# A long convolution by matrix transforms: from 64 by 64 points on the whole array to 128 by 32 points on its four quarters

## The chip, the cores and the metric

The kernel runs on one core of one Trainium2 chip. The metric is device time in microseconds, the median of several runs. The names in the traces are PE for TensorE, PEld for TensorE's weight loads, DVE for VectorE, ACT for ScalarE, POOL for GpSimd and SP for SyncE, which issues nearly all DMAs here.

## The reference

Sequence length 2048, 512 channels, all in fp32. Two kinds of layer alternate, A B A B, each after a layer norm over the channels, each with a long causal convolution per channel:

```python
def _A_ref(q, k, v, shift_k, ssm_k, ssm_D):
    ...                                   # k_shift: short causal convolution of k, 4 taps
    kv = k_shift * v
    y = irfft(rfft(kv padded to 2S) * rfft(ssm_k padded to 2S))[:S]
    y = y + kv * ssm_D
    return q * y
def _B_ref(u, log_A_real, A_imag, C_real, C_imag, log_dt, D_skip):
    ...
    P = jnp.exp((A * dt[:, None])[:, :, None] * pos[None, None, :])
    K = 2.0 * jnp.einsum("dn,dnl->dl", C, P).real      # 128 modes a channel, 2048 taps
    y = irfft(rfft(u padded) * rfft(K padded))[:L]
    return y + u * D_skip
x = x + _A_ref(_layernorm(x), A_k, A_v, A_shift_k, A_ssm_k, A_ssm_D)
x = x + _B_ref(_layernorm(x), B_...)
x = x + _A_ref(_layernorm(x), ...)                    # the same weights, k and v again
x = x + _B_ref(_layernorm(x), ...)
return x
```

The convolution inside layer A does not depend on x, so it is done once and its result is used twice. There are three long convolutions in all (A's, and B's twice), and two spectra of kernels (A's given taps, B's generated taps).

## The kernel before, in words

**Transform.** A 4096-point real transform is done in two matrix steps. The first step (`fwd_rows`, `fwd_group`, L171; tile `pf`) multiplies 128-partition data by a constant 128 by 128 matrix. In layer A, in both spectra, and in the first groups of layer B that matrix is `wz`, half of whose rows are zeros, so that each of the two halves of the partitions is picked out in turn; elsewhere in layer B 64-row halves of `w1` are used. VectorE transposes the result in blocks (L193, L195) into `z`. The second step (`f2_chunk`, L200; tile `pu`) multiplies by one 128 by 128 matrix of `w2` for each of 32 frequencies, four frequencies a chunk, 8 chunks a quarter of 128 channels. `spectrum_quarter` does both steps for a kernel's taps, adds `D` as a bias to tap 0 by a one-row matmul (L187), copies the chunks out of PSUM (L245, tile `pc`) and stores them in DRAM (`spec`, L246).

**Product and inverse.** `convolution` walks over 32 chunks (4 quarters of channels by 8). For each it loads the chunk of the spectrum twice, real part and imaginary part on all partitions (`kab`, L260), runs `f2_chunk`, has ScalarE make a swapped and negated copy of `pu` in two halves (`sw`, L277 and L278), VectorE multiply `pu` by `kab` (`vv`, L279), GpSimd multiply `sw` by `kab` (L281), and GpSimd or, every third time in layer B, VectorE add the two (L282). `lag` chunks later the inverse's first step (L291; tile `pi`) multiplies `vv` by `mm`, ScalarE copies it to `ie` (L292), VectorE transposes (L306, tile `w`), and the last step (L312; tile `po`, two 64-column tiles of the array) is followed by `finish`.

**Order.** Two generators of program steps are interleaved by `run_steps`. `stream` makes layer B's taps (64 steps of `mags`, `angles`, `waves`, `products`, `contract`; L467 to L520) and, as each quarter is complete, its spectrum. `diagonal` makes layer A's spectrum, the gated input (`gated`), and runs layer A's convolution. Then `gated_update` applies A to x (L715 to L724), layer B's convolution runs, `gated_update` again, and layer B's convolution for the second time, ending with the stores of `out` (L816). Within an engine a scheduler places the instructions by its own timeline, so `pu`, `pf` and the generator's matmuls mix.

**Buffers.** While A's convolution and the generator run, PSUM has three banks for `pf`, `pu`, `pi` and `po` (tag `c1`), two for `pm` and the second spectrum, two for `pa` and one for `pk`. In layer B there are four banks for `pu`, `pi`, `po` and two double banks for `pf`.

Of the kernel before, what the change touches and what calls it, by code (L numbers as in the profile page):

```python
# [20 lines left out]
NQ = 4  # L21
CK = 4
NCH = 32 // CK
# [8 lines left out]

def dft_constants():
    c = lambda t: np.cos(2 * np.pi * t)
    s = lambda t: np.sin(2 * np.pi * t)
    n1 = np.arange(32)
    k2 = np.arange(64)
    j = np.arange(32)
    n2 = [32 * (j // 16) + 16 * b + j % 16 for b in range(2)]
    w1 = np.zeros((2, 32, 2, 2, 32))  # L40
    w4 = np.zeros((2, 2, 32, 2, 32))
    w2 = np.zeros((32, 2, 2, 32, 2, 64))
    for b in range(2):
        w1[b, :, b, 0, 0] = 1
        w1[b, :, b, 1, 0] = (-1.0) ** n1
        w4[b, 0, 0, b] = 1 / NFFT
        w4[b, 1, 0, b] = (-1.0) ** n1 / NFFT
        m = n2[b][:, None]
        for k in range(1, 32):
            w1[b, :, b, 0, k] = c(n1 * k % 64 / 64)  # L50
            w1[b, :, b, 1, k] = -s(n1 * k % 64 / 64)
            w4[b, 0, k, b] = 2 * c(n1 * k % 64 / 64) / NFFT
            w4[b, 1, k, b] = -2 * s(n1 * k % 64 / 64) / NFFT
            ph = m * (k + 64 * k2)[None, :] % NFFT / NFFT
            w2[k, b, 0, :, 0], w2[k, b, 0, :, 1] = c(ph), -s(ph)
            w2[k, b, 1, :, 0], w2[k, b, 1, :, 1] = s(ph), c(ph)
        for q in range(32):
            ph = m[:, 0] * (64 * q) % NFFT / NFFT
            w2[0, b, 0, :, 0, q] = c(ph)
            if q > 0:  # L60
                w2[0, b, 0, :, 1, q] = -s(ph)
            ph = m[:, 0] * (32 + 64 * q) % NFFT / NFFT
            w2[0, b, 1, :, 0, 32 + q], w2[0, b, 1, :, 1, 32 + q] = c(ph), -s(ph)
        w2[0, b, 0, :, 1, 0] = (-1.0) ** m[:, 0]
    w2 = w2.reshape(32, 128, 128)
    mm = w2.transpose(0, 2, 1).copy()
    mm[0].reshape(2, 64, 128)[:, 1:] *= 2.0
    w1 = w1.reshape(64, 128)
    f = lambda a: np.ascontiguousarray(a, dtype=np.float32)
    return {  # L70
        "w1": f(np.concatenate([w1, w1])),
        "w2": f(w2.transpose(1, 0, 2)),
        "mm": f(mm.transpose(1, 0, 2)),
        "w4": f(w4.reshape(128, 64)),
    }
# [24 lines left out]
def kernel(ctx: ExitStack, tc: tile.TileContext, out, x_in, kv_in, ssmk_in, ssmd_in,  # L100
                           la_in, ai_in, cr_in, ci_in, ldt_in, ldtb_in, dsk_in,
                           w1_in, w2_in, mm_in, w4_in, minus_in, tt_in, tg1_in, tg2_in, dbg=None):
# [12 lines left out]
    spec = [[dram.tile([NCH, 128, CK * 128], F32, name=f"spec{i}_{q}") for q in range(NQ)] for i in range(2)]  # L115
# [7 lines left out]
    LV = 0  # L123
# [11 lines left out]
    wz = cpool.tile([128, 2, 128], F32, name="wz")  # L135
    w2 = cpool.tile([128, 32, 128], F32, name="w2")
    mm = cpool.tile([128, 32, 128], F32, name="mm")
# [5 lines left out]
    psum, w1, swapped = {}, [], [None]  # L143

    def bank(name, tag="c1"):
        pool, bufs = psum[tag]
        return pool.tile([128, 512], F32, name=name, tag=tag, bufs=bufs)


# [4 lines left out]
    def wide_bank():  # L154
        pool, bufs = psum["f1"]
        return pool.tile([128, 2, 512], F32, name="pf", tag="f1", bufs=bufs).rearrange(
            "p a (x t r) -> p a x t r", t=16, r=2)


    def fwd_rows(src, pf, j, step, rows, full):  # L160
        for a in (1, 0):
            half = slice(0, 128) if full else slice(64 * a, 64 * a + 64)
            w = wz[:, a, :] if full else w1[0][half, :]
            rhs = src(half, j, step)[:, rows, :]
            o = pf[:, a].rearrange("p x t r -> p t x r")[:, rows]
# [5 lines left out]
            yield T.matmul(o, w, rhs, start=True, stop=True)  # L171

    def fwd_group(src, z, c0, n, step, tap0=None, first=None, tag="c1", full=True, early=None):
        for j in range(0, n, step):
            rest = slice(0, 16)
            if early is not None:
                pf, rest = early, slice(8, 16)
            elif step == 32:
                pf = wide_bank()
            else:  # L180
                both = bank("pf", tag).rearrange("p (x n r) -> p x r n", n=32, r=2)
                pf = both.rearrange("p x r (a t) -> p a x t r", a=2)
            for i in fwd_rows(src, pf, j, step, rest, full):
                if first is not None:
                    after(i, first)
            if tap0 is not None:
                T.matmul(pf[:, 0, :, 0, :], wz[0:1, 0, :],  # L187
                         tap0[:, j:j + step].rearrange("p (x r) -> p x r", r=2), start=False, stop=True,
                         skip_group_check=True)
            zr = z[:, (c0 + j) // 2:(c0 + j + step) // 2].rearrange("p x k r -> p x r k")  # L190
            if step == 32:
                for r in range(2):
                    V.transpose(zr[:, :, r], pf[..., r].rearrange("p a x t -> p x a t"))  # L193
# [722 lines left out]
```

## Time and profile before

| | |
|---|---|
| median of 3 runs | 797.05 us (791.2 to 798.05) |
| the profiled execution | 802.01 us, its span 800.2 us |
| mean granted TensorE clock | 0.862 of full |
| DMA | 135.49 MB, mean 169 GB/s |

The profile lists each engine's busy time, groups of instructions by line with their mean duration, and a chain of work that ended last. One matmul of fp32 data appears as two PE instructions and two weight loads, so a chunk of four matmuls is "x8". A group's mean duration includes the time an instruction waits in the array's pipeline behind its predecessor; the spacing of starts is shorter, and is read from pieces of the chain.

### The profile page before, as it was taken

The page shows a single profiled execution, that of the slowest core. Times are in us where ns is not written, and L with a number is a line of the kernel's source. Part 1 is how long each engine was busy: PE and PEld are TensorE (multiplying, and loading weights), DVE is VectorE, ACT ScalarE, POOL GpSimd, SP SyncE. Part 2 cuts the span into 40 slices and gives each one's busy share as a digit, 9 for nine tenths or more (in the row PEclk, how much of TensorE's full clock was granted, in tenths as well). Part 3 has the DMA queues.
Part 4 walks back from the last instruction along what each step waited for, and adds up shares of the span by engine and source line. Part 5 has one row for each costly group of instructions (what it writes and reads, how often), then busy time and mean ns, then how long its engine had stood idle before and what let it go on. Part 6 is the DMA issues. An engine that isn't in the chain of part 4 may idle for free.

```text
span 800.2 us, 14659 instructions
## 1 busy us (share of the span) xinstructions
PE 676.5 (85%) x5192; PEld 475.6 (59%) x5192; DVE 604.8 (76%) x939; ACT 479.2 (60%) x881; POOL 531.9 (66%) x464
## 2 busy tenths in 40 slices
PE   3779988999989999999899867889789840898996
PEld 2555755667667766757666444666557720476673
DVE  7767856989996958756849699625568989878775
ACT  4144443535478884785884687628746625878572
POOL 4966744967868975777964678206666836288783
PEclk9686765869999999999999755699989975999998
DMA  9586254557378463664541891238968541078792
GB/s 329 195 263 249 94 174 151 187 171 253 130 222 231 131 184 97 192 187 153 125 119 54 268 313 42 76 115 206 238 169 197 147 106 53 1 182 220 200 247 99
DMA packets 89614, 135.49 MB, mean 169 GB/s; under 512 B 8509, under 2 KB 37701, under 8 KB 89029
## 3 DMA queue, kind: packets, MB, share of 16 engines
q1 hardware_dynamic: 88644, 132.13, 56.8%
q0 software_dynamic: 896, 2.43, 1.0%
q8 instruction: 41, 0.67, 0.4%
q14 instruction: 33, 0.26, 0.1%
HBM read 98.87 MB, written 35.65 MB: 168 GB/s over the span
## 4 chain that ended last, share of the span: by engine, by line
PE 27%; DVE 14%; ACT 4%; DMA 4%; issue 3%; POOL 2%; SPq 1%; DVEq 0%; POOLq 0%; ACTq 0%
PE pu L200 8%; PE pf L171 6%; PE pi L291 5%; PE po L312 5%; DVE x L722 3%; DVE ut L715 2%; DMA kab<-spec 2%; POOL sw L281 1%; DMA yaq<-ya_d 1%; DVE w L306 1%; PE pk L520 1%; DVE vv L279 1%; POOL vv L282 1%; DVE tt L506 1%; DVE st L822 1%
## 5 line engine op out<-in xcount | busy, mean ns | idle before, releaser
L281 POOL TENSOR_TENSOR sw<-sw,kab 128x512 f32<-128x512 f32 x96 | 125.4, 1313 | 76.5 <-ACT sw L278 65.5
L505 POOL TENSOR_TENSOR xy<-tt,m 128x512 f32<-128x512 f32 x64 | 89.7, 1402 | 62.7 <-ACT tt L494 54.6
L200 PEld LDWEIGHTS pu<-zu,w 128*128 128x128 f32 x768 | 94.6, 191 | 51.1 <-DVE vv L279 18.4
L200 PE MATMUL pu<-zu,w 128*128 128x128 f32 x768 | 108.4, 283 | 12.2 <-DVE vv L279 11.8
L171 PE MATMUL pf<-kk,wz 128*128 128x256 f32 x256 | 96.2, 512 | 24.7 <-DMA kk<-ssmk_in 15.9
L279 DVE TENSOR_TENSOR vv<-pu,kab 128x512 f32<-128x512 f32 x96 | 64.7, 679 | 64.6 <-ACT sw L278 32.0
L282 POOL TENSOR_TENSOR vv<-vv,sw 128x512 f32<-128x512 f32 x76 | 100.1, 1320 | 14.8 <-DVE vv L279 12.0
L291 PE MATMUL pi<-vv,mm 128*128 128x128 f32 x768 | 106.9, 284 | 3.4 <-DVE vv L279 2.8
L291 PEld LDWEIGHTS pi<-vv,mm 128*128 128x128 f32 x768 | 95.3, 195 | 15.9 <-issue 9.4
L277 ACT ACTIVATE sw<-pu 64x512 f32<-64x512 f32 x96 | 57.1, 595 | 63.0 <-PE pu L200 52.1
L200 PE MATMUL pu<-zk,w 128*128 128x128 f32 x512 | 80.4, 313 | 5.5 <-DVE zk L195 3.6
L492 ACT ACTIVATE tt<-pa 128x512 f32<-128x512 f32 x64 | 38.5, 601 | 75.4 <-PE pa L484 64.1
L200 PEld LDWEIGHTS pu<-zk,w 128*128 128x128 f32 x512 | 74.8, 223 | 14.4 <-DVE zk L195 4.1
L171 PEld LDWEIGHTS pf<-kk,wz 128*128 128x128 f32 x256 | 57.8, 247 | 42.8 <-issue 16.0
L245 ACT COPY pc<-pu 128x512 f32<-128x512 f32 x64 | 37.5, 592 | 63.1 <-PE pu L200 45.7
L469 ACT ACTIVATE m<-pm 128x512 f32<-128x512 f32 x96 | 54.2, 598 | 31.5 <-PE pm L467 30.6
L506 DVE TENSOR_TENSOR tt<-tt,m 128x512 f32<-128x512 f32 x64 | 71.6, 1118 | 0.4
L507 DVE SCALAR_TENSOR_TENSOR xy<-tt,m 128x256 f32<-128x256 f32 x64 | 51.1, 798 | 24.0 <-ACT tt L493 20.2
L195 DVE STREAM_TRANSPOSE zk<-pf 128x512 f32<-128x512 f32 x64 | 44.5, 703 | 28.0 <-PE pf L187 27.8
L312 PE MATMUL po<-w,w 128*64 128x512 f32 x192 | 56.1, 671 | 7.8 <-DVE w L306 6.7
L509 POOL TENSOR_TENSOR xy<-tt,m 128x256 f32<-128x256 f32 x64 | 60.9, 951 | 0.0
L520 PE MATMUL pk<-xy,tt 128*32 128x64 f32 x2048 | 53.7, 244 | 5.8 <-POOL xy L509 3.1
(141 smaller groups left out, 1310.3 us busy)
## 6 DMA issues: line engine op xcount, KB each, us to landing
kab<-spec SPq DMA_DIRECT2D x188, 256.0 KB, 4.0
spec<-pc SPq DMA_DIRECT2D x64, 256.0 KB, 2.4
kvt<-kv_in SPq DMA_DIRECT2D x16, 624.0 KB, 6.5
yaq<-ya_d SPq DMA_DIRECT2D x8, 1024.0 KB, 5.5
kk<-ssmk_in SPq DMA_DIRECT2D x16, 256.0 KB, 5.1
kv_d<-u SPq DMA_DIRECT2D x16, 256.0 KB
kdram<-ks SPq DMA_DIRECT2D x64, 64.0 KB, 2.4
kk<-kdram SPq DMA_DIRECT2D x16, 256.0 KB, 2.6
```

The source lines that it names most:

```text
L171: yield T.matmul(o, w, rhs, start=True, stop=True)
L200: ins = T.matmul(pu[:, i, :], w2[:, c * CK + i, :], z[:, :, c * CK + i, :], start=True, stop=True)
L277: S.mul(sw[0:64], pu[64:128], -1.0)
L279: V.tensor_mul(vv, pu, kabs[s][:, 0])
L281: (V if last else G).tensor_mul(sw, sw, kabs[s][:, 1])
L282: (V if last or s % add_dve == add_dve - 1 else G).tensor_add(vv, vv, sw)
L291: i1s[t] = T.matmul(pi[:, i, :], mm[:, c * CK + i, :], vvs[t][:, i, :], start=True, stop=True)
L312: ins = T.matmul(po[64 * a:64 * a + 64], w4, ws[g][:, :, 16 * a:16 * a + 16, :].rearrange("p x t r -> p t x r"), start=True, stop=True, ti ...
L505: G.tensor_mul(xy[:, :, :, 32:64], tt[:, :, :, 1:33], m1[:, :, 32:64][:, None].to_broadcast([128, 2, 8, 32]))
L506: (G if (4 * gi + k) % E2P == E2P - 1 else V).tensor_mul(e2, e2, m2[:, None].to_broadcast([128, 2, 8, 32]))
L509: (V if (4 * gi + k) % XLP == XLP - 1 else G).tensor_mul(xy[:, 0, :, 0:32], tt[:, 0, :, 0:32], m1[:, :, 0:32])
L520: T.matmul(pk[32 * i4:32 * i4 + 32, 2 * k + i, :], e2[:, r, 4 * i + i4, :], xy[:, r, 4 * i + i4, :], start=r == 0, stop=r == 1, tile_posit ...
```

## The change

The transform's factors become 128 by 32, evaluated at frequencies k + 1/2, so that no frequency is purely real and every matrix of the second step is a full complex one. The first step uses 64-row halves of one matrix `w1` everywhere (two matmuls of 512 columns a group in place of four of 256), the second step is 64 matrices of 64 by 64 a quarter, each in one quarter of the array: four matmuls with different `tile_position` follow each other, and write two banks by two halves of the partitions. A chunk now has 8 frequencies (1024 columns, two banks), so there are 16 chunks a convolution in place of 32.

The product's two parts are no longer added: `vv` and `sw` both go to TensorE, which multiplies them by `ma` and `mb` and accumulates in PSUM. ScalarE's swapped copy becomes one plain copy of the whole chunk, and the fix-ups of `kab` for frequency 0 are gone.

```diff
-            S.mul(sw[0:64], pu[64:128], -1.0)
-            swapped[0] = S.copy(sw[64:128], pu[0:64])
-            V.tensor_mul(vv, pu, kabs[s][:, 0])
-            (V if last else G).tensor_mul(sw, sw, kabs[s][:, 1])
-            (V if last or s % add_dve == add_dve - 1 else G).tensor_add(vv, vv, sw)
+            swapped[0] = S.copy(sw, pu)
+            V.tensor_mul(vv, pu, kabs[n][:, 0])
+            G.tensor_mul(sw, sw, kabs[n][:, 1])
...
-                for i in range(CK):
-                    i1s[t] = T.matmul(pi[:, i, :], mm[:, c * CK + i, :], vvs[t][:, i, :], start=True, stop=True)
+                pi, i1s[n] = i1_chunk(vvs[n], c)
...
+    def f2_chunk(z, c, first=None):
+        pu = banks("pu").rearrange("p (u i c) -> p u i c", u=2, i=4)
+        for i in range(4):
+            for u in range(2):
+                for h in range(2):
+                    k = 8 * c + 4 * h + i
+                    ins = T.matmul(pu[64 * h:64 * h + 64, u, i, :], w2[64 * u:64 * u + 64, k, :],
+                                   z[64 * u:64 * u + 64, :, k, :], start=True, stop=True, tile_position=(64 * u, 64 * h))
+    def i1_chunk(parts, c):
+        pi = banks("pi").rearrange("p (h i c) -> p h i c", h=2, i=4)
+        for i in range(4):
+            for n, (table, part) in enumerate(zip((ma, mb), parts)):
+                for h in range(2):
+                    for u in range(2):
+                        ins = T.matmul(pi[64 * u:64 * u + 64, h, i, :], table[64 * h:64 * h + 64, 8 * c + 4 * u + i, :],
+                                       part[64 * h:64 * h + 64, u, i, :], start=n == 0, stop=n == 1,
+                                       tile_position=(64 * h, 64 * u), skip_group_check=True)
```

Loads and stores whose rows stand in another order than the new transform wants them (`kk` of layer A's taps, `kvt`, `xt`, `x`, and the stores of `out`) are issued as four DMAs of 32 partitions each:

```diff
+    def quadrants(dma, tile_, array, store=False):
+        for i, j in enumerate((0, 2, 1, 3)):
+            pair = tile_[32 * i:32 * i + 32], array[32 * j:32 * j + 32]
+            dma(*(pair[::-1] if store else pair))
```

PSUM is divided anew. During A's convolution and the generator two double banks (tag `c2`) serve `pf`, `pu`, `pi` and `po` of A and of both spectra, three banks (tag `pt`) serve `pm` and `pa` together; in layer B there are three double banks and two single ones. Buffers of `kab`, `vv` and `sw` hold 1024 columns: 2 of each in A (3, 2 and 2 of 512 before), 3 of each in B (4, 5 and 5 before), and `ut` in the gated update has 2 of its own in place of 3. `spectrum_quarter` yields 8 times in place of 12.

More of the change, by code (lines that the diff above doesn't have):

```diff
@@ L21 @@
 NQ = 4
-CK = 4
-NCH = 32 // CK
+NCH = 8
+NCK = 4
 MAGIC = 1.5 * 2.0**23
@@ L170, in fwd_rows @@
                 rhs = rhs.rearrange("p t (x r) -> p t x r", r=2)
[L171 to L193, printed above, removed]
-            else:
-                V.transpose(zr, both)
@@ L342 @@
     nc.sync.dma_start(flat(ai), ai_in)
[L343 to L346 removed]
+    nc.sync.dma_start(w1, w1_in)
     dt2 = gp.tile([128, NQ, 32], F32, name="dt2")
@@ L727, in gated_update @@
                 for _ in range(WX if t == 15 else 1):
-                    T.matmul(bank("idle")[:, 0:WN], wz[:, 0, :], x[:, t, 0:WN], start=True, stop=True)
+                    T.matmul(bank("idle")[:, 0:WN], w1, x[:, t, 0:WN], start=True, stop=True)
             yield t
```

264 lines of the change are left out of this document (122 added, 142 removed).

## The prediction

> **What bounds the kernel now.** I read the page's engine line first, then the busy time of each engine by stage (windows), then the chain of work that ended last, then the timeline of TensorE at single places.
>
> ```profile
> PE 676.5 (85%) x5192; PEld 475.6 (59%) x5192; DVE 604.8 (76%) x939; ACT 479.2 (60%) x881; POOL 531.9 (66%) x464
> core 0: us, PE busy (x) PEld busy (x) DVE busy (x) ACT busy (x) POOL busy (x), PEclk, DMA share, GB/s
> 0.00:80.00 80.00, 53.90 (x237) 37.41 (x238) 58.90 (x75) 30.04 (x50) 52.71 (x54) 0.77 0.76 259
> 80.00:440.00 360.00, 338.40 (x3047) 241.40 (x3046) 276.46 (x387) 222.98 (x386) 259.36 (x217) 0.89 0.53 159
> 440.00:500.00 60.00, 43.28 (x400) 28.64 (x399) 53.56 (x85) 46.17 (x92) 45.09 (x34) 0.64 0.68 208
> 500.00:545.00 45.00, 38.46 (x275) 29.18 (x273) 20.93 (x44) 23.05 (x52) 7.01 (x12) 0.83 0.38 111
> 545.00:655.00 110.00, 92.54 (x578) 65.58 (x576) 81.06 (x149) 64.29 (x117) 73.73 (x67) 0.92 0.72 176
> 655.00:690.00 35.00, 10.90 (x24) 4.35 (x24) 34.62 (x100) 20.12 (x51) 19.40 (x19) 0.61 0.20 50
> 690.00:800.00 110.00, 99.03 (x640) 69.05 (x640) 79.29 (x107) 72.58 (x138) 74.59 (x66) 0.98 0.64 173
> ```
>
> The stages: start-up; generator with layer A's convolution (to 440); first gated update with the generator's rest (to 500); the generator's last spectrum (to 545); first B convolution; second gated update; second B convolution. TensorE fills 94% of 80 to 440 and 90% of the last stage. VectorE fills the gated updates (89% and 99%). In the B convolutions the chain confirms it: it runs from one TensorE piece to the next.
>
> ```profile
> 703.09 1.09 PE pu L200 x8
> 704.18 1.03 PE pi L291 x8
> 705.21 0.89 PE pu L200 x8
> 706.10 1.06 PE pf L171 x4
> 707.16 1.09 PE pi L291 x8
> 708.25 1.06 PE pf L171 x4
> 709.31 1.09 PE pu L200 x8
> 710.40 0.89 PE pi L291 x8
> ```
>
> A chunk of eight 128-column instructions takes 0.89 us behind another such chunk (111 ns an instruction) and 1.09 behind `pf`: a change of the array's shape costs about 0.2.
>
> **The price of the new matmuls.** No row of before shows a quarter of the array. Its two ingredients have rows, at full clock:
>
> ```profile
> 302.40 0.65 PE L520 MATMUL pk<-xy,tt 128*32 128x64 f32 x32
> 261.84 1.89 PE L171 MATMUL pf<-u,wz 128*128 128x256 f32 x8
> 739.74 1.99 PE L171 MATMUL pf<-u,w 64*128 64x512 f32 x8
> 302.08 0.39 PE L187 MATMUL pf<-dr,wz 1*128 1x16 f32 x2
> ```
>
> `pk` uses four column tiles in turn with new weights each time: 32 instructions in 0.65 us, so 20 ns each, although one alone streams 64 columns, half of the 111 ns that 128 take. So four column tiles run at once, weight loads included. `pf` on 64-row halves: eight instructions of 512 columns in 1.99, while eight of 256 columns on the whole array take 1.89. Twice the columns in the same time: two row tiles run at once. I take both together: four quarters cost one 128-column instruction, 111 ns, 28 ns each. The bounds are 20 ns (the `pk` row) and 111 (no overlap at all); nearest is the `pk` row, since it too has four tiles.
>
> F2: a new chunk has 32 instructions, 8 fours by 0.111 is 0.89, with the shape change 1.09. It replaces two old chunks of 1.06 (the mean of the L200 pieces above is near 1.0): 32 old chunks by 1.06 are 34, 16 new by 1.09 are 17.4, saving 16.5 a convolution. The inverse: 64 instructions, 16 fours by 0.111 plus 0.1 is 1.9, against two old chunks of 0.95: nothing gained or lost. The addition that GpSimd and VectorE did is thus free on TensorE. Together 96 instructions replace 32 that took about 4 us, so the change loses on TensorE from 39 ns an instruction on.
>
> [...]
>
> First step: a group of 32 channels on `wz` takes 1.89 (x8, row above); on row halves x4 takes 1.06 (chain). Saved 0.85 to 0.95; 32 groups of spectra, 16 of layer A. The tap-0 matmul comes once a group instead of twice: 0.33 each.
>
> **Layer B, second time (690 to 800).** F2 gives -16.5. Other engines, by these groups:
>
> ```profile
> L281 POOL TENSOR_TENSOR sw<-sw,kab 128x512 f32<-128x512 f32 x96 | 125.4, 1313 | 76.5 <-ACT sw L278 65.5
> L282 POOL TENSOR_TENSOR vv<-vv,sw 128x512 f32<-128x512 f32 x76 | 100.1, 1320 | 14.8 <-DVE vv L279 12.0
> L279 DVE TENSOR_TENSOR vv<-pu,kab 128x512 f32<-128x512 f32 x96 | 64.7, 679 | 64.6 <-ACT sw L278 32.0
> L277 ACT ACTIVATE sw<-pu 64x512 f32<-64x512 f32 x96 | 57.1, 595 | 63.0 <-PE pu L200 52.1
> L278 ACT COPY sw<-pu 64x512 f32<-64x512 f32 x96 | 55.5, 578 | 1.1
> L292 ACT COPY ie<-pi 128x512 f32<-128x512 f32 x64 | 37.3, 582 | 13.8 <-PE pi L291 12.9
> 690.00:800.00 110.00, 11.80 (x10) 28.83 (x22) 0.98 0.64 173
> ```
>
> (The last row is L282 alone: VectorE 11.80, GpSimd 28.83.) GpSimd loses 28.8, VectorE 11.8 and some 2 of start-up cost as instructions double in length, ScalarE half of 32 x 1.17, about 20. All this lies beside TensorE: it takes VectorE from 79 to 65 and GpSimd from 75 to 46 in a stage that shrinks to 94, so TensorE (99 - 16.5 = 82) still sets the end, and these savings I cost at nothing. The ends of the stage get longer: the first and last chunk are twice as long. On the way from `pu` to `ie` the last copy takes about 1.0 in place of 0.58, the inverse 1.9 in place of 0.95, the GpSimd product as much as product and sum before: +1.4. The last output is four DMAs, three more issues:
>
> ```profile
> L816 SPq DMA_DIRECT2D out_dram<-yo x16: 332/348/545, 734.0 to 796.7; - x16
> L230 SPq DMA_DIRECT2D kk<-ssmk_in x16: 327/333/2271, 5.9 to 166.2; - x16
> ```
>
> 3 x 0.35 is +1.0. Net -14. The spectrum's loads keep their bytes and their count (four of 256 KB for 1024 columns), with rows of 4 KB instead of 2.
>
> ```profile
> kab<-spec SPq DMA_DIRECT2D x188, 256.0 KB, 4.0
> ```
>
> Loading is one large chunk ahead instead of three small ones, some 6 us for a landing of 4.0; the DMA share of 0.64 leaves room. If that cover is gone, each late load holds VectorE's L279, behind which the transposes for `pf` and `w` are queued, and TensorE behind them: up to 4 us a time.
>
> **Layer B, first time.** The same -16.5, +1.4, no stores: -15.
>
> **To 545.** At full clock TensorE loses, to 440: first step 38 (about 24 groups of spectra and A's 16), tap 0 8, the spectra's F2 23 (25 old pairs of chunks by 2.0 to 1.09), A's F2 16.5. Together 86, and at the clock of 0.89 some 92 of 392. It won't all come: VectorE keeps 276 of 360, GpSimd 217 after losing A's additions. And PSUM gets narrower: each bank pair of `pu` is held for the matmuls (1.1), ScalarE's copy (1.0) and VectorE's product (1.2), which waits for ScalarE as L279's row shows; with only two such pairs for everything, TensorE waits where it ran ahead on three banks. The bounds are 0 and 92; I take half, -46, halfway because VectorE at the 94% that TensorE had would allow 66.
>
> The interleaving moves work: with fewer yields in the spectra, the changed kernel's TensorE order has 46 of 64 generator steps ahead of A's last inverse matmuls, before 52. Six steps fall into the VectorE-bound update:
>
> ```profile
> L506 DVE TENSOR_TENSOR tt<-tt,m 128x512 f32<-128x512 f32 x64 | 71.6, 1118 | 0.4
> L507 DVE SCALAR_TENSOR_TENSOR xy<-tt,m 128x256 f32<-128x256 f32 x64 | 51.1, 798 | 24.0 <-ACT tt L493 20.2
> L483 DVE TENSOR_SCALAR y<-pa 128x512 fp32r<-128x512 f32 x64 | 42.7, 672 | 3.7 <-PE pa L479 3.7
> ```
>
> 6 x 2.6 us is +15. The last spectrum (500 to 545) stands on the chain with TensorE alone after two DMA waits:
>
> ```profile
> 515.39 4.46 DMA kdram<-ks
> 519.93 2.57 DMA kk<-kdram
> 525.38 2.79 PE pf L171 x12
> 528.17 3.64 PE pu L200 x32
> 532.47 2.07 PE pu L200 x16
> ```
>
> Its four groups lose 0.85 each and the tap, its eight chunks half of 7.6: -8. Start-up:
>
> ```profile
> L171 PE MATMUL pf<-kk,wz 128*128 128x256 f32 x256 | 96.2, 512 | 24.7 <-DMA kk<-ssmk_in 15.9
> ```
>
> TensorE waits for `kk` there; ahead of the third `kk` stand 12 more DMAs, at 0.33 a piece 4 us, of which I take half as hidden by the two tiles ahead of it: +2. The other four-way loads issue beside TensorE; SP has room. Sum to 545: -46 + 15 - 8 + 2 = -37.
>
> **Sum.** 802 (the profiled execution, span 800.2) - 37 - 15 - 14 = 736. The profiled execution is 0.6% above the median of 797.05; in those terms 731.
>
> **The rivals.**
> 1. *Slower: the quarters run only two at once*, since before shows row pairs and column fours, never both. Then 55 ns: 96 instructions take 5.5 instead of 4 a chunk, +25 a convolution and +27 with the ends. A's loss cancels its first-step gain, and the spectra's F2 is even. 802 + 54 is 856, in median terms 851. It decides from 39 ns an instruction; one at a time would be above 1000. Against it: the two rows that each show full overlap.
> 2. *The gain comes only in layer B*: PSUM's two pairs and VectorE hold the first 500 us. 802 - 8 - 29 + 2 = 767, so 762. For it: ScalarE and VectorE empty each `pu` in turn. [...]
> 3. *The clock falls.* It stood at 0.64 and 0.61 where TensorE had gaps (window rows). At 0.75 in layer B (0.95 before) its 82 become 104 and a stage gains 5 instead of 14; with the saving to 440 halved to 23 as well: 736 + 19 + 23 = 778, so 773.
> 4. *All of it comes*: 92 to 440 and the moved steps hidden in idle VectorE time: 802 - 92 - 8 - 29 + 2 = 675, so 671.
>
> **How the numbers follow.** Forecast 0.57 (705 to 755 by itself, from a quarter to three quarters of the 92), rival 1 0.13, rival 2 0.16, rival 3 0.08, rival 4 0.06. The range takes in the forecast and rivals 2 and 3 and stops short of the whole of rival 4: 695 to 785. Slower by over 1%, which is about what a measurement can tell from no change, is rival 1: 0.13; within 1% are the ends of rivals 2 and 3: 0.04; faster is the rest, 0.83.
>
> **What would show it.** Fours of `pu` and `pi` starting together, 32 in about 0.9 and 64 in 1.8; TensorE near 82 in the last stage and still on the chain; L282 gone; VectorE above 80% to 440, and the update from 440 longer. Wrong: `pi` pieces of over 2.5, waits of `pu` or `pf` on ScalarE or VectorE adding up to tens of us, or a clock below 0.85 in layer B.

## The result, and the profile after

| | before | after |
|---|---|---|
| median of the runs shown side by side | 795.46 us (791.2 to 798.05, 4 runs) | 873.37 us (872.31 to 873.67, 4 runs) |
| ratio, 95% interval | | 1.098 [1.093, 1.104] |
| span of the profiled execution | 800.2 us | 870.2 us |

The change costs 78 us. I had forecast a gain of 66. A ratio that stands with its interval leaves out executions in a slower state, 1.5% or more above the fastest of their kernel.

The page of the changed kernel: its engine line, two lines of its chain, and two rows of its DMA issues (the last number is the median from issue to landing, in us):

```profile
PE 589.4 (68%) x8504; PEld 351.0 (40%) x8504; DVE 572.7 (66%) x871; ACT 407.5 (47%) x659; POOL 419.6 (48%) x307
...
PE 23%; DVE 22%; DMA 17%; issue 14%; ACT 9%; POOL 8%; SPq 8%; DVEq 0%; POOLq 0%; ACTq 0%
DMA kab<-spec 5%; SPq L145 5%; PE pu L187 4%; PE pi L200 4%; PE pf L165 4%; PE po L308 3%; DMA kvt<-kv_in 3%; DVE tt L496 3%; DVE x L711 2%; PE pm L457 2%; POOL sw L279 2%; DMA xt<-x_in 2%; PE pk L510 2%; DVE zu L178 2%; DVE ut L704 2%
...
kab<-spec SPq DMA_DIRECT2D x184, 256.0 KB, 6.3
kk<-ssmk_in SPq DMA_DIRECT2D x64, 64.0 KB, 3.2
```

TensorE lost 87 us of work (676.5 to 589.4) and every other engine lost work too, yet the span grew by 70. No engine is above 68%. In the chain stand three things: waiting for `kab`, the issue of the four-way DMAs by SP (L145), and "issue". The chain of the kernel before can be followed back only to 358 us, so the two are compared from 360 us on: there `kab` went from 2.9% to 8.3%, "issue" from 6.2% to 16.7%, and L145, which is new, has 2.0%.

Where the time went is read by stage. The edges below are each kernel's own marks, rounded: first generator contraction `pk`; first `pu` of layer A's convolution; its last `po`; first `pu` and last `po` of the first B convolution; the same of the second. First the kernel before, then the changed one (start:end, length, then busy time of PE, PEld, DVE, ACT, POOL with instruction counts, granted TensorE clock, DMA share, GB/s):

```profile
75.00:233.00 158.00, 144.98 (x1212) 101.78 (x1204) 130.47 (x189) 73.19 (x127) 110.69 (x88) 0.75 0.53 170
233.00:443.00 210.00, 201.26 (x1912) 144.18 (x1912) 151.84 (x208) 155.24 (x270) 154.71 (x135) 0.99 0.52 147
443.00:537.00 94.00, 70.74 (x607) 51.00 (x607) 67.71 (x117) 59.63 (x122) 47.66 (x41) 0.69 0.54 164
537.00:653.00 116.00, 100.54 (x627) 70.64 (x625) 82.94 (x144) 71.36 (x132) 75.21 (x66) 0.93 0.72 178
697.00:796.00 99.00, 93.87 (x620) 67.02 (x620) 73.05 (x96) 65.58 (x120) 74.14 (x65) 0.98 0.69 184
```

```profile
103.00:282.00 179.00, 122.45 (x1303) 67.34 (x1301) 122.05 (x177) 69.89 (x108) 99.09 (x77) 0.88 0.51 149
282.00:459.00 177.00, 151.83 (x2688) 91.73 (x2684) 118.60 (x160) 114.19 (x171) 92.70 (x66) 0.92 0.62 159
459.00:610.00 151.00, 84.73 (x949) 48.41 (x945) 90.30 (x146) 83.18 (x160) 62.36 (x52) 0.59 0.49 124
610.00:714.00 104.00, 85.87 (x1648) 56.59 (x1648) 71.36 (x119) 40.81 (x54) 40.38 (x18) 0.89 0.81 173
758.00:862.00 104.00, 84.05 (x1648) 56.34 (x1644) 60.51 (x68) 41.76 (x57) 40.37 (x18) 0.89 0.72 165
```

Stage by stage, by the marks themselves, the changed kernel is 29 us later at the first `pk`, loses 20 in the spectra, gains 33 in layer A's convolution, loses 58 from there to layer B, gains 12 in the first B convolution, and loses 5 in the second. So it is 73 us late at the start of layer B, and layer B as a whole is no help. In the first stage TensorE does 22 us less work in 21 us more time. By the generator's marks the same 73 us are: first `pk` 29 later, the time from the first to the last `pk` 36 longer (437 to 473), and from the last `pk` to layer B 9 longer.

What TensorE waited for in that first stage, before (75 to 233, first three rows) and after (103 to 282, five of its rows; total us, times, longest):

```profile
PE pa L484 <- DVE y L483: 4.0, 4, 2.7
PE pf L171 <- DVE zk L195: 3.2, 2, 1.7
PE pa L479 <- ACT tt L493: 2.7, 2, 2.6
```

```profile
PE pa L474 <- DVE y L473: 13.9, 7, 3.2
PE pk L510 <- POOL xy L499: 8.7, 3, 4.2
PE pu L187 <- DVE zk L178: 6.8, 2, 6.3
PE pf L165 <- DVE zk L178: 4.9, 1, 4.9
PE pk L510 <- POOL tb L600: 4.6, 1, 4.6
```

Before, TensorE had work of its own to do while the generator's values went through ScalarE, VectorE and GpSimd. After, it stands in its queue at `pa` and `pk` until they come back.

The quarters themselves do what was priced. Pieces of the chain in the first B convolution (start, us, what):

```profile
617.21 7.01 DMA kab<-spec
...
624.34 1.22 DVE vv L278
625.56 1.23 DVE zu L178 x2
...
632.66 1.04 PE pu L187 x32
...
671.01 1.75 PE pi L200 x64
```

Thirty-two quarter instructions take 1.04 us behind `pf`, the change of shape included, where I had 1.09, and the inverse's sixty-four 1.75, where I had 1.9. But a chunk's load of 7.0 us stands ahead of them, on the chain.

### The profile page after: what moved, and what is told of

It is laid out like the page before. It is cut to its first block, busy times and chain, and to the rows that moved or that the text cites. A ratio compares the mean times of both kernels' runs of the same rounds, so it can differ in the third digit from the quotient of the medians.

```text
span 870.2 us, 20836 instructions
## 1 busy us (share of the span) xinstructions
PE 589.4 (68%) x8504; PEld 351.0 (40%) x8504; DVE 572.7 (66%) x871; ACT 407.5 (47%) x659; POOL 419.6 (48%) x307
## 4 chain that ended last, share of the span: by engine, by line
PE 23%; DVE 22%; DMA 17%; issue 14%; ACT 9%; POOL 8%; SPq 8%; DVEq 0%; POOLq 0%; ACTq 0%
DMA kab<-spec 5%; SPq L145 5%; PE pu L187 4%; PE pi L200 4%; PE pf L165 4%; PE po L308 3%; DMA kvt<-kv_in 3%; DVE tt L496 3%; DVE x L711 2%; PE pm L457 2%; POOL sw L279 2%; DMA xt<-x_in 2%; PE pk L510 2%; DVE zu L178 2%; DVE ut L704 2%
## 5 line engine op out<-in xcount | busy, mean ns | idle before, releaser
L279 POOL TENSOR_TENSOR sw<-sw,kab 128x1024 f32<-128x1024 f32 x48 | 114.3, 2382 | 176.1 <-ACT sw L277 144.9
L165 PE MATMUL pf<-kk,w 64*128 64x512 f32 x128 | 63.5, 1033 | 68.6 <-DMA kk<-kdram 20.7
L200 PE MATMUL pi<-vv,ma 64*64 64x128 f32 x1536 | 88.2, 288 | 9.1 <-DVE vv L278 4.7
L200 PE MATMUL pi<-sw,mb 64*64 64x128 f32 x1536 | 87.8, 285 | 7.2 <-issue 6.5
L278 DVE TENSOR_TENSOR vv<-pu,kab 128x1024 f32<-128x1024 f32 x48 | 58.4, 1218 | 45.1 <-ACT sw L277 36.7
L187 PE MATMUL pu<-zk,w 64*64 64x128 f32 x1024 | 66.8, 381 | 22.8 <-DVE zk L178 19.2
L187 PE MATMUL pu<-zu,w 64*64 64x128 f32 x1536 | 64.3, 304 | 24.7 <-DVE zu L178 13.9
L178 DVE STREAM_TRANSPOSE zu<-pf 128x512 f32<-128x512 f32 x96 | 62.2, 690 | 24.6 <-PE pf L165 24.5
L200 PEld LDWEIGHTS pi<-vv,ma 64*64 64x64 f32 x1536 | 59.2, 143 | 15.7 <-issue 7.9
L200 PEld LDWEIGHTS pi<-sw,mb 64*64 64x64 f32 x1536 | 60.8, 143 | 9.2 <-issue 8.2
```

Of the source, the lines that this page charges most:

```text
L165: yield T.matmul(o, w1[half, :], rhs, start=True, stop=True)
L178: V.transpose(zr[:, :, r], pf[..., r].rearrange("p b x t -> p x b t"))
L187: ins = T.matmul(pu[64 * h:64 * h + 64, u, i, :], w2[64 * u:64 * u + 64, k, :], z[64 * u:64 * u + 64, :, k, :], start=True, stop=True, til ...
L200: ins = T.matmul(pi[64 * u:64 * u + 64, h, i, :], table[64 * h:64 * h + 64, 8 * c + 4 * u + i, :], part[64 * h:64 * h + 64, u, i, :], star ...
L278: V.tensor_mul(vv, pu, kabs[n][:, 0])
L279: G.tensor_mul(sw, sw, kabs[n][:, 1])
```

## The experiments

### The loads of layer B

Leave the loads out (the first chunks' spectra are used again). `a_noload`:

```diff
+            if which == 1 and n >= nk:
+                kabs[n] = kabs[n - nk]
+                return
```

> The changed kernel, but both B convolutions load the spectrum only for their first three chunks and use these again for the other thirteen (the output leaves the right spectrum out). Changed kernel: first B convolution 103 us from its first pu to its last po (610.4 to 713.4), second 104 (757.8 to 861.9), with TensorE busy about 80 in each. Theory 1 (the loads of kab, four DMAs into 32 partitions each with rows of 4 KB, hold layer B): both fall to 80 to 90, the whole by 28 to 45 us, to some 830 to 845. Rival (the path pu, copy, product, pi with three buffers and two chunks of lag holds it): both stay above 97, the whole within 12 us of the changed kernel.

> The kernel before with the same leaving-out: layer B's loads only for the first four small chunks of each convolution. Before: 115 us (537.1 to 652.4) and 99 us (696.9 to 795.9). Theory 1: before was held by its loads in a few places only (chain: 7.9 and 5.1 us of kab), so it gains 5 to 15 in the first and 2 to 6 in the second, 7 to 20 in all. If its B convolutions fall by as much as the changed kernel's do, the loads are no worse after the change and the loss there lies elsewhere.

Measured: 838.32 us for the changed kernel without the loads (873 with), 788.17 for the kernel before without them (801.61 with; lowest against lowest 774.22 and 790.91, so 13 to 17 us; its few fix-ups of `kab` on GpSimd go with the loads). The B convolutions without their loads, of the changed kernel, then of the one before:

```profile
609.00:699.00 90.00, 78.14 (x1648) 50.63 (x1648) 71.01 (x119) 40.45 (x53) 40.50 (x18) 0.96 0.18 48
742.00:829.00 87.00, 78.71 (x1648) 51.20 (x1648) 61.30 (x70) 42.51 (x59) 40.57 (x18) 0.94 0.18 42
```

```profile
537.00:639.00 102.00, 95.95 (x633) 68.85 (x631) 81.10 (x144) 71.18 (x132) 72.98 (x57) 0.97 0.22 59
683.00:780.00 97.00, 92.92 (x622) 66.50 (x620) 72.94 (x96) 66.00 (x121) 72.25 (x56) 1.00 0.10 36
```

Without loads the new transform is worth 12 and 10 us in layer B, near the 15 and 14 of the prediction. With them the changed kernel pays 14 and 18 (103 to 89, 104 to 86, from first `pu` to last `po`), the kernel before 14 and 3 (115 to 101, 99 to 96). So the loads cost no more than before in the first convolution and 15 us more in the second, whose gain they eat.

Is it the bytes, or the shape of the DMAs? A first try put each load on 64 partitions, with the source repeated twice by a leading dimension of stride zero, alone (`a_kab`) and with the single DMAs of the next part (`a_both`):

```diff
-                    p0 = 64 * h + 32 * r
                     (G if first_b and n < GL else nc.sync).dma_start(
-                        kab[p0:p0 + 32].rearrange("p r u i c -> p r (u i c)"), src[h])
+                        kab[64 * h:64 * h + 64, r].rearrange("p u i c -> p (u i c)"),
+                        src[h][:, r, :][None].to_broadcast([2, 32, 1024]))
```

> The changed kernel with kab's four DMAs a chunk cut otherwise: each fills 64 partitions with one row of 4 KB instead of 32 partitions with two rows; bytes, packets and number of DMAs stay. Theory 3 (writing into 32 partitions is slow): the 4 KB packets of kab fall from a median near 300 ns to 170 to 200, the landing from 6.3 to near 4.5 us, and each B convolution is 5 to 12 us shorter: 850 to 863. Theories 1 and 2: no difference, 873.

> Both edits together, one DMA for each load and kab by 64 partitions. Theories 1 and 3 together: their gains add up, 800 to 815. Theory 2: 850 or more.

Measured: 1539.71 us (ratio 1.94) and 1527.30. It says nothing of 32 against 64 partitions, since it brought a cost of its own. Issues of `kab` in this kernel (ns least/median/most), and 200 us of its second B convolution (columns as above):

```profile
L262 SPq DMA_DIRECT2D kab<-spec x184: 475/4116/19370, 192.0 to 1493.7; - x184
...
1300.00:1500.00 200.00, 51.42 (x908) 35.73 (x906) 32.90 (x39) 20.18 (x26) 23.61 (x10) 0.62 0.17 59
```

SP is blocked 4.1 us per issue at the median (0.43 in the changed kernel), a load lands after 16.4 us (6.3), and only 0.17 of the sixteen engines' time is used in this stretch, while the loads are what everything waits for: over the whole run GpSimd's products 514 us, VectorE's 381. What makes a load in this form so slow, no run shows.

A second try kept the bytes loaded and made the shape right: the spectrum of layer B is stored twice, as `kab` has it, by eight small stores, and one DMA loads a chunk into all 128 partitions. `a_dup`:

```diff
...
+                for p in range(4):
+                    for e in range(2):
+                        row = 64 * (p // 2) + 32 * e
+                        nc.sync.dma_start(spec[which][q][c][row:row + 32, 1024 * (p % 2):1024 * (p % 2) + 1024], pc[32 * p:32 * p + 32])
...
+            if which == 1:
+                (G if first_b and n < GL else nc.sync).dma_start(kab.rearrange("p r u i c -> p (r u i c)"), spec[which][q][c])
```

> The changed kernel with the spectrum of layer B stored twice, in the arrangement that kab has, so that one DMA of 128 partitions by 8 KB loads a chunk in place of four of 32 partitions; the bytes loaded are the same, the bytes stored before layer B are doubled. Theory 1 in its sharp form (the 32-partition shape costs, through slow packets and four issues): the second B convolution falls from 104 us to 86 to 94, near the 86 that it took without the loads, and the first from 103 to 89 to 96. Rival (the bytes cost, whatever the shape): both stay above 98. The time to layer B grows by up to 15 us through 128 smaller stores.

Measured: 856.49 us, ratio to the kernel before 1.069 [1.062, 1.075]; the changed kernel's was 1.098. Its B convolutions, and the loads of its second one:

```profile
618.00:709.00 91.00, 78.59 (x1648) 51.47 (x1648) 71.17 (x119) 39.93 (x52) 40.42 (x18) 0.96 0.61 208
752.00:844.00 92.00, 79.99 (x1648) 52.71 (x1648) 61.20 (x70) 42.68 (x59) 40.45 (x18) 0.94 0.57 187
```

```profile
kab<-spec SPq DMA_DIRECT2D x13, 1024.0 KB, 5.4
```

The bytes are the same, and the convolutions fall from 103 and 104 to 90 and 91 us, 1 and 5 above no loads at all. (Layer B itself starts 8 us later, at 618.7 instead of 610.4; the spectrum's small stores come ahead of it.) So it was the shape: 128 partitions, rows of 8 KB and one DMA a chunk, against 32 partitions, rows of 4 KB and four DMAs. Which of the three it was, no run separates. The rows of the last stage, four fifths of whose bytes are these loads, say by how much: the share times 16 engines over the rate is 0.72 x 16 / 165 = 70 ns of engine time per KB in the changed kernel's last stage, 0.57 x 16 / 187 = 49 here, and 0.69 x 16 / 184 = 60 before the change. A whole chunk of 1 MB lands in 5.4 us, where a quarter of one took 7.0 in the same stage:

```profile
kab<-spec SPq DMA_DIRECT2D x52, 256.0 KB, 7.0
```

The loads before the change, into 64 partitions, stand at 60 ns per KB, between the 70 and the 49, but the lengths of the rows differ as well (2, 4 and 8 KB).

### The four-way DMAs

`a_one` gives `kk`, `kvt`, `xt`, `x` and the output back their single DMAs (the rows are laid out in that order beforehand); `b_four` splits them in the kernel before.

```diff
-        for i, j in enumerate((0, 2, 1, 3)):
-            pair = tile_[32 * i:32 * i + 32], array[32 * j:32 * j + 32]
-            dma(*(pair[::-1] if store else pair))
+        pair = tile_, array
+        dma(*(pair[::-1] if store else pair))
...
```

> The changed kernel with each load and store of kk, kvt, xt, x and out as one DMA of 128 partitions again (the rows are put in the new order when the input arrays are laid out, and the output's back). Theory 1 (the fourfold DMAs through SP's queue delay the generator and the gated input): the first convolution matmul of layer A comes near 240 instead of 282 us, and the time falls by 40 to 55 us, to about 820 to 830. Theory 2 (narrower PSUM, two kvt buffers and the new order of steps cost the time before layer B): it falls by 10 us at most, 863 or more. Theory 3 (the loads of kab into 32 partitions): no more than the 4 us of the out stores.

> The kernel before with kk of layer A, kvt, xt, x and out each loaded or stored by four DMAs of 32 partitions, in the same order of rows; nothing else changes. Theory 1: 35 to 50 us slower, 830 to 845, with layer A's first convolution matmul late by that. Theories 2 and 3: within 10 us of before.

Measured: `a_one` 856.43, ratio 1.078 [1.064, 1.093], start of layer B 595 instead of 610; `b_four` 822.44 against 804.06, ratio 1.027 [0.995, 1.059], lowest against lowest 808.89 and 791.4; with that interval it settles nothing by itself, and goes the same way. So the splitting costs some 17 us, not the 40 and more that I had expected when I saw SP's queue so full.

> The last one together with single DMAs in place of four for kk, kvt, xt, x and the output. If the two parts are independent their gains add: single DMAs took the kernel from 873 to 856, so this is some 15 us below the last one, at 825 to 845, and still above the 797 of before, since the PSUM part is untouched.

Measured: 835.36, ratio 1.042 [1.037, 1.048]. The two DMA parts add: 17 and 17 give 38. It is the best form of the changed kernel that I found, and it is still 33 us slower than the kernel before (802.07 beside it). The rest lies ahead of layer B, which starts at 599 in it; both B convolutions are shorter than before (88 and 94 us).

### The 600 us ahead of layer B

Four theories were tried: PSUM, the order of the work, the scheduler's reordering, and the input loads. The first was PSUM: before, three banks in rotation for layer A, two each for `pm` and `pa`, the generator's spectra in those of `pm`; after, two pairs for all of it and three banks for `pm` and `pa`. Done to the kernel before, whole (`b_psum`) and in its two parts (`b_c12`, `b_pt`):

```diff
-    psum["c1"] = (pp, 7 - NPA - NPM)
...
+    psum["c1"] = (pp, 2)
...
-        pm = pp.tile([128, 512], F32, name="pm", tag="pm", bufs=NPM)
+        pm = pp.tile([128, 512], F32, name="pm", tag="pt", bufs=3)
...
-        pa = pp.tile([128, 512], F32, name="pa", tag="pa", bufs=NPA)
+        pa = pp.tile([128, 512], F32, name="pa", tag="pt", bufs=3)
...
-                    todo.append(spectrum_quarter(1, m // 16, kdram, kp, zlast_k, 1, "pm"))
+                    todo.append(spectrum_quarter(1, m // 16, kdram, kp, zlast_k, 1, "c1"))
```

> The kernel before with PSUM turned as narrow in number as after: two banks in rotation for everything but the generator (it had three, and the generator's spectra used the two of pm), and three shared by pm and pa (it had two and two). Theory 2 (two PSUM tiles for all of spectra, layer A and generator spectra cost the time before layer B): the first B convolution starts 30 us or more later than the 537 of before, the whole is 25 to 45 us longer. Rival (PSUM is not what holds it): under 10 us.

> The kernel before with two banks in place of three in the rotation that layer A's spectra, its convolution and its output share; pm, pa and the generator's spectra keep theirs. With all of the narrowing (two for everything, three shared by pm and pa) it had become 68 us longer. If the shared rotation is the part that costs, this alone is 30 to 60 us longer than before, and layer A's convolution takes 235 to 255 us instead of 210; if it is the generator's banks, under 12.

> The kernel before with three banks shared by pm, pa and the generator's spectra in place of two and two; the rotation of three for layer A stays. If the generator's banks are the part that costs, 30 us or more longer than before; if it is the rotation of layer A, within 12 us.

Measured: `b_psum` 869.39 against 801.61 (lowest against lowest 852.56 and 790.91, so 62 to 68 us); `b_c12` ratio 1.044 [1.038, 1.051], 37 us; `b_pt` 1.017 [1.011, 1.024], 14 us. Layer A's convolution in `b_psum`:

```profile
273.00:525.00 252.00, 209.65 (x1879) 143.86 (x1880) 146.16 (x193) 149.70 (x252) 153.61 (x133) 0.89 0.41 110
```

252 us for what took 210 (265 in `b_c12`), and layer B starts at 604 instead of 537. Not one matmul differs, so the narrower PSUM alone costs the kernel before about as much as the whole change costs ahead of layer B. But the size is all that agrees. In `b_psum` the generator's contractions end early, at 445 instead of 512; its chain to layer B runs through layer A's convolution, which ends at 525 instead of 443, and then through the generator's last spectra, which stand behind it. In the changed kernel it is the other way round: layer A's convolution is 33 us shorter than before, and the contractions themselves end late, at 576. TensorE's waits in its first stage say the same: 1.7 us for ScalarE's copies out of PSUM and 4.9 for the transposes of `pf`, against 34 at `pa` and `pk`. So `b_psum` is no evidence that PSUM holds the changed kernel. Its price also includes that the scheduler places instructions otherwise when there are fewer banks.

The converse, in the changed kernel: free each pair sooner (`a_early`), or share out the eight banks otherwise (`a_c3`).

```diff
-                V.tensor_mul(vv, pu, kabs[n][:, 0])
+                V.tensor_mul(vv, sw, kabs[n][:, 0])
```

```diff
-    psum["c2"] = (pp, 2)
...
+    psum["c2"] = (pp, 3)
...
-        pm = pp.tile([128, 512], F32, name="pm", tag="pt", bufs=3)
+        pm = pp.tile([128, 512], F32, name="pm", tag="pt", bufs=1)
```

(`pa` likewise.)

> The changed kernel with VectorE's product reading sw, ScalarE's copy of pu, in place of pu itself, so that the PSUM pair is free after the copy, about 1.2 us sooner a chunk; GpSimd's product then waits for VectorE's, 1.2 us later a chunk. Theory 2 (two PSUM pairs hold the time before layer B): layer A's convolution falls from 176 us (281.8 to 458.3) by 10 or more, and layer B, which has three pairs and is late on GpSimd's product anyway, gets no shorter or up to 10 longer. Rival (the pairs are not held by VectorE's product): A's convolution within 5 us of 176 or longer.

> The changed kernel with the eight PSUM banks shared out otherwise before layer B: three pairs for spectra and layer A, one bank for pm and pa (two pairs and three). Theory 2 says that both sides are short: A's last output comes 20 us or more earlier than 458, the generator's end 20 or more later than 577, and the whole is no better, 865 to 910. If neither side is held by PSUM both marks move by under 10 us and the whole stays.

Measured: `a_early` 873.35, layer A's convolution 176 us as in the changed kernel: VectorE's product is not what holds the pairs, or GpSimd's later product takes back what it frees. `a_c3` 1011.94: layer A did not end earlier but at 512, against my expectation, and the generator ends 148 us later. The generator's contractions (ns least/median/most, first and last start) in the kernel before, the changed one and `a_c3`:

```profile
L520 PE MATMUL pk<-xy,tt x2048: 216/219/316, 74.5 to 511.6; 128*32 128x64 f32 x187
```

```profile
L510 PE MATMUL pk<-xy,tt x2048: 216/314/318, 103.4 to 576.3; 128*32 128x64 f32 x187
```

```profile
L510 PE MATMUL pk<-xy,tt x2048: 216/314/317, 143.4 to 724.9; 128*32 128x64 f32 x187
```

From the first to the last `pk` the 64 generator steps run for 437, 473 and 582 us. So with one bank for `pm` and `pa` the generator is what everything waits for, and a third pair is worth nothing to layer A beside that.

The order of the work (`a_order`: two yields a chunk, so that the steps mix as before; `a_prog` and `b_prog`: `schedule_with_timeline_sim=False`, each engine in program order):

```diff
             nc.sync.dma_start(spec[which][q][c], pc)
             yield
+            if which == 0:
+                yield
...
```

> The changed kernel with layer A's spectra yielding twice after each of their four large chunks, one step of the gated products a yield and the row statistics at the places that they had before: the order of the work is that of before again. Theory 3 (the order: spectra and gated products pressed into 16 generator steps instead of 24, so that 18 generator steps in place of 12 are left behind layer A) expects the first B convolution to start at 570 to 590 instead of 610, and the whole 20 to 40 us shorter, at 835 to 855. Theory 2 (PSUM) expects within 8 us of the changed kernel, since the same work goes through the same two PSUM pairs.

> The changed kernel with each engine's instructions in the order in which the program writes them, without the compiler's own reordering by its estimates. Theory 4 (its estimates misjudge quarter matmuls, and the order that it makes is the loss): 20 us or more shorter than the changed kernel, below 850, while the same on the kernel before brings nothing. Theory 2 (PSUM): no gain, 870 to 920.

> The kernel before in the program's own order. The reordering must be worth something to it: 800 to 840. If it is worth much more here than in the changed kernel (difference of the two over 20 us), the reordering is part of the loss; if both lose alike, it is not.

Measured: `a_order` 873.21, the changed kernel's time to the microsecond, though layer A's convolution ends at 478 instead of 458; `a_prog` 1015.17, `b_prog` 890.61. The scheduler helps both kernels, the changed one more (142 against 90), so its reordering is not the loss. That the order of the steps is not the loss is shown only in part: in the trace of `a_order` 16 generator steps are still left behind layer A, where the changed kernel has 18 and the kernel before 12.

The input loads (`a_noin`, `b_noin`: fourteen of the sixteen `kvt` loads, thirteen of them before the change, and all `xt` loads left out):

```diff
-            kvt = ap.tile([128, 39, 32], F32, name="kvt", tag="kab", bufs=NKA)
-            quadrants(nc.sync.dma_start, kvt.rearrange("p t c -> p (t c)"), kv_in[grp])
+            kvt = kvts[grp] = kvts[grp - NKA] if grp >= NKA else ap.tile([128, 39, 32], F32, name="kvt", tag="kab", bufs=NKA)
+            if grp < NKA:
+                quadrants(nc.sync.dma_start, kvt.rearrange("p t c -> p (t c)"), kv_in[grp])
...
-            xt = ap.tile([128, 512], F32, name="xt", tag="kk", bufs=3)
-            quadrants(nc.sync.dma_start, xt, x_in[:, t, :])
-            V.bn_stats(st0[:, t, :], xt)
+            V.bn_stats(st0[:, t, :], w2[:, 0:8].rearrange("p k c -> p (k c)"))
```

> The changed kernel with kvt loaded for the first two groups only, which the other fourteen use again, and with the row statistics taken from a resident table instead of loaded tiles of x (the right gated product and statistics are left out). Theory 5 (these loads, late behind two kvt buffers and 128 issues of quadrants in SP's queue, hold the products in order and the generator behind them): the first pu of layer A falls from 282 to 250 or less and the start of layer B from 610 to 585 or less. Rival (PSUM and the generator's own chain hold it): the first pu stays above 270, the start of layer B above 598.

> The same leaving-out in the kernel before, with its three kvt buffers. Theory 5: its loads were hidden, so the first pu of layer A stays within 12 us of 233 and the start of layer B within 10 of 537. If it gains as much as the changed kernel, the loads cost both alike and explain nothing of the difference.

Measured: 874.75 and 806.83; neither differs from its own kernel. The stage up to layer A did become shorter in `a_noin`:

```profile
110.00:274.00 164.00, 119.39 (x1283) 64.94 (x1285) 116.70 (x140) 65.37 (x103) 89.31 (x69) 0.59 0.35 106
452.00:617.00 165.00, 94.81 (x1085) 53.97 (x1084) 102.23 (x163) 93.20 (x177) 72.15 (x62) 0.58 0.46 117
```

The first took 164 us instead of 179, half of it because it began 7 us later, and the stage from layer A to layer B 165 instead of 151: given back, because the generator's steps, which end it, came no sooner (last `pk` at 582). The first `pu` of layer A at 274 and layer B at 617 are what the rival expected. `b_noin` missed its expectation in one point: the first `pu` of layer A came at 194, 39 us earlier than before, but that convolution then took 251 us instead of 210, and layer B started at 542. What sets the start of layer B in the changed kernel is the generator, not layer A.

What holds the generator stays open; the traces say where it falls behind. Its ninth step's first `pk` comes at 145 us before and at 197 after, 52 us late, which is most of the 65 by which the last `pk` is late. The next 40 steps take 280 and 287 us, the last 16 take 87 and 92. The stretch of the first eight steps, before and after (columns as above):

```profile
75.00:145.00 70.00, 64.30 (x467) 44.24 (x463) 47.53 (x67) 28.27 (x49) 42.99 (x34) 0.61 0.43 139
```

```profile
103.00:197.00 94.00, 59.55 (x547) 32.19 (x544) 65.38 (x85) 28.78 (x43) 64.56 (x47) 1.00 0.57 163
```

After, VectorE and GpSimd have 18 and 22 us more to do in this stretch, and the chain in it goes through SP's four-way issues (18% of the stretch) and the loads of `xt` and `kvt` (11% and 10%). No run took all of that away: the ninth step comes at 188 us with single DMAs (`a_one`) and at 194 without most of the loads (`a_noin`); in `a_order` it comes at 179, but the seventeenth at 259, as in the changed kernel.

A second difference between the two is in `pu` of the spectra up to layer A, before and after (ns least/median/most):

```profile
L200 PE MATMUL pu<-zk,w x224: 269/272/581, 87.6 to 225.6; 128*128 128x128 f32 x112
```

```profile
L187 PE MATMUL pu<-zk,w x438: 266/412/473, 102.6 to 279.1; 64*64 64x128 f32 x146
```

Before, half of these ran within 3 ns of the least duration; after, half took 1.5 times the least or more. `pk` shows the same, 219 and 314 at the median. TensorE has gaps now and its instructions run slow, and the generator's chain goes through TensorE several times a step. The two `pa` of a step in the same stage, before and after (busy us and mean ns behind the bar):

```profile
L479 PE MATMUL pa<-tt,rw 64*128 64x512 f32 x22 | 12.8, 586 | 2.7 <-ACT tt L493 2.7
L484 PE MATMUL pa<-y,minus 128*128 128x512 f32 x22 | 12.4, 564 | 4.0 <-DVE y L483 4.0
```

```profile
L474 PE MATMUL pa<-y,minus 128*128 128x512 f32 x21 | 14.5, 717 | 13.9 <-DVE y L473 13.9
L469 PE MATMUL pa<-tt,rw 64*128 64x512 f32 x19 | 11.0, 808 | 0.0
```

Together 1.53 us instead of 1.15, so 0.38 a step, where the generator is longer by 36 us over 64 steps, 0.56 a step. But the slow instructions are not shown to be what makes it longer, and `a_order` speaks against it. Its contractions:

```profile
L512 PE MATMUL pk<-xy,tt x2048: 217/243/317, 107.3 to 577.3; 128*32 128x64 f32 x187
```

Their median, 243 ns, is nearer the least again, and the median of its `pa` on `tt` over the whole run is 502 ns, where the kernel before has 498 and the changed one 789. Its generator still takes 470 us. Nor does the granted clock follow the durations: it is 0.75 in this stage before, 0.88 in the changed kernel and 0.59 in `a_noin`, whose generator takes as long. That PSUM's narrowing makes the gaps in the changed kernel is not shown either.

## Why the prediction was wrong, step by step

The span was forecast to fall by 66 us and grew by 70. Of these 136 us, 110 lie ahead of layer B (forecast -37, measured +73), 3 in the first B convolution, 19 in the second and 4 behind it.

- *Quarters at 28 ns an instruction, four at once*: right. 32 take 1.04 us, 64 take 1.75; rival 1 (only two at once, 851) came near the time for a reason that did not happen.
- *Layer B, -15 and -14*: the transform is worth 12 and 10 without loads. It came in the first convolution (115.3 to 103.1 us from first `pu` to last `po`), and not in the second (99.0 to 104.1), through the term that failed next. One reading behind it was too wide: before, the chain of the first B convolution runs from one TensorE piece to the next only from 582 us on, and up to there through GpSimd's product and sum and one load of 7.9 us.
- *"The spectrum's loads keep their bytes and their count ... the DMA share of 0.64 leaves room", costed at nothing*: wrong for the second convolution. The bytes were kept, but the shape was not: 32 partitions instead of 64, rows of 4 KB instead of 2. Against no loads it costs 18 us there, where the kernel before pays 3; with one DMA into 128 partitions the two convolutions are 13 and 14 us shorter (`a_dup`). I had even priced a late load, up to 4 us a time, and then left it out of the sum.
- *"The other four-way loads issue beside TensorE; SP has room", and +2 at the start*: wrong, 17 us (`a_one`), 15 of them ahead of layer B. I priced the issue in SP's queue at one place only. Of the 29 us by which the first `pk` is late, single DMAs give back 5; the rest is not explained.
- *To 545, -46, halfway between 0 and 92*: this is the step that failed most. I took TensorE's work to be the path to layer B, so that work taken from it would bring layer B nearer, as far as VectorE and the PSUM pairs would let it, and at worst leave it where it was. TensorE did lose the work (72 us less between the first `pk` and the end of layer A's convolution), and that convolution gained its 33 us, but the start of layer B is 73 us late, because the path to it is the generator, whose last `pk` comes 65 us later. That TensorE at 94% set the pace held for the kernel before; I did not ask what comes next when it has less to do, and the case of a loss was open. What makes the generator late stays open: most of it is there by 197 us, single DMAs for the input give back 15 us, and the PSUM pairs, which I had named as the brake, did not keep layer A's convolution from getting shorter. (The 92 was a slip too: 86 at a clock of 0.89 are 97.)
- *+15 for six moved steps*: the six steps did move: 18 are left behind layer A's last `po` where 12 were, and from there to the last `pk` it is 118 us where it was 69. With two of them moved back (`a_order`, 99 us) the whole was no shorter, so as far as that goes it moves time about and does not cost it.
- *-8 for the last spectrum*: from the last `pk` to layer B's first `pu` it is 34 us where it was 25. The spectrum's own TensorE pieces did get shorter (10 us from 590.9 to 601.1, before 15 from 522.6 to 537.3), but the last taps came back from DRAM 13 us after they were made instead of 8.5, and layer B's first `pu` stood 9 us behind the spectrum instead of beside it.
- *Rival 3, the clock*: I gave it layer B. Layer B's clock fell a little (0.98 to 0.89, and back to 0.94 without the loads); the spectra, ahead of layer B, are where TensorE's instructions ran slow.

## What to carry to other kernels

When the engine that fills a stage loses a good part of its work, ask what the next limit is in latency, not in busy time: in the stages before and behind layer A's convolution all engines were below 70%, and a chain through four of them, the generator's, set the start of layer B. A change that doubles the size of a tile halves how many there are. Narrowing the buffers of the kernel at hand tells beforehand whether it is sensitive to that; but here the time so found fell in another stage than the changed kernel's loss, so compare the places, not only the sums. And a DMA that keeps its bytes but not its partitions, rows and number is a new DMA (the loads of layer B: 103 and 104 us in one shape, 90 and 91 in the other): price it as one.

## What the runs showed of the hardware

- Four 64 by 64 quarters of the array do run at once: 32 instructions of 128 columns behind `pf` in 1.04 us, 33 ns each with the change of shape in it, and 64 in 1.75, 27 ns each, where the kernel before took 111 ns for one such instruction on the whole array.
- The last stage used 70 ns of engine time per KB with loads into 32 partitions, rows of 4 KB and four DMAs a chunk, 49 with loads into 128 partitions, rows of 8 KB and one DMA a chunk (estimates from shares and rates of all its traffic, above).
- With each load of `kab` into 64 partitions, its source repeated twice by a leading dimension of stride zero, an issue took 4.1 us at the median instead of 0.43, a load landed after 16.4 us instead of 6.3, and the whole took 1540 us instead of 873.
